# Placing the side matmuls of the full-attention layers by an estimate of two engines' clocks

## The chip, the core and the metric

The kernel runs on one NeuronCore of a Trainium2 chip. The metric is the device time of one execution in microseconds (us); lower is better. Five engines run their own instruction queues in order: TensorE (PE in the profile, its weight loads PEld), VectorE (DVE), ScalarE (ACT), GpSimd (POOL) and SyncE (SP, which here only issues transfers). An engine waits for another through semaphores, and whatever stands behind a waiting instruction in its queue waits too.

## The reference

Four pre-norm attention layers follow each other on a sequence of 2048 rows of 512 features, with 32 heads of 16 features. Layers 0 and 2 attend within a window of 256 keys, layers 1 and 3 to all keys. There is no MLP.

```python
def _B_ref(x, wqkv, wo):
    qkv = (x @ wqkv).reshape(B, S, 3, H, Dh).transpose(2, 0, 3, 1, 4)
    q, k, v = qkv[0], qkv[1], qkv[2]
    scores = jnp.einsum("bhqd,bhkd->bhqk", q, k) * Dh ** -0.5
    p = _softmax(scores, axis=-1)
    o = jnp.einsum("bhqk,bhkd->bhqd", p, v)
    return o.transpose(0, 2, 1, 3).reshape(B, S, D) @ wo
# _A_ref is the same with scores outside 0 <= query - key < 256 masked out
x = x + _A_ref(_layernorm(x), A_wqkv, A_wo)     # layer 0
x = x + _B_ref(_layernorm(x), B_wqkv, B_wo)     # layer 1
x = x + _A_ref(_layernorm(x), A_wqkv, A_wo)     # layer 2
x = x + _B_ref(_layernorm(x), B_wqkv, B_wo)     # layer 3
```

## The kernel before

**A full layer.** Layers 1 and 3 work through 32 *quads* each: four heads (`qd`) by 512 queries (`c`). A quad takes 16 steps `j` of 128 keys. In each step TensorE computes two groups of scores (eight matmuls each, L771, tile `s`, two buffers), ScalarE turns each group into exponentials with one activation of 128x1024 (L779, tile `e`, five buffers), and TensorE later multiplies the exponentials of the step with the values (16 matmuls, L896, into the two banks `acc`; below "the value product"). Within a step TensorE's order is: first group of scores, value product of two steps before, second group of scores, and then whatever side work has been placed there. The value product is held in a list `pvq` that `flush` empties.

**The thirty-second group.** In most quads one group of scores (step `DJ`, placed last in its quad) does not go to ScalarE: `unit` (L787) computes it into `b`, VectorE turns it into an integer (L793), and GpSimd evaluates the exponential with a polynomial (L810 to L817). Such a quad has 31 activations, the others 32. `units` decides when `unit` may run.

**Side work.** The projections of later blocks (keys `keys`, queries `queries`, values `values`), the output projections (`wo`, `wo_part`) and the layer norms of the layers around run beside the attention. Their matmuls (L424) write one shared pair of PSUM banks, tile `b`, with a single buffer in the full layers. A *piece* is one pair of operands in `mms`: eight matmuls of 512 columns, planned as `MM` = 0.222 us. Twelve pieces (in `wo_part`, three) fill `b`; then VectorE reads it (`join`, or L718 and L693 for `x`), and only then may the next user write `b`. Users of `b` are the pieces, `unit`, and `squares` (L579, the sums of squares that bound the scores).

**What sets the order.** The order on TensorE, VectorE and GpSimd in the full layers is written while the program is built: nothing is rescheduled later. The planner keeps an estimated time `clock[0]` (TensorE), `vt_` (VectorE), `pt_` (GpSimd), and `PH["free"]`, the time from which `b` is taken to be readable and free. A step of the attention counts as `PH["step"]`, 1.8 us (0.9 for the step with the unit). `Side.share` decides after each group of scores how many pieces follow: it hands out a `budget` that spreads the remaining cost evenly over the remaining steps, and keeps a `lag` account (+0.222 per piece, -0.48 per step) that limits a run to one or two pieces more. `Side.finish` runs what is left at the end of a block (layer 3), or of the layer (layer 1), with no attention beside it. `settle` runs `squares` when their time has come, and `project` calls it before its first piece. `epilogue` ends a quad: VectorE reads `acc` (L440, L441, tile `sa`) before the next quad's first value product may overwrite it.

## Time and profile before

| | us |
|---|---|
| median of 3 runs (2795.52 to 2798.0) | 2796.48 |
| the profiled execution's own time | 2797.65 |
| its span in the profile | 2795.9 |
| ScalarE busy over the span | 2330.1 (83%) |
| TensorE busy over the span | 2500.0 (89%) |
| VectorE, GpSimd busy | 1445.5 (52%), 1537.5 (55%) |
| layer 1, first to last activation | 499 to 1457 |
| layer 3, first to last activation | 1812 to 2777 |
| GpSimd exponentials (L793) | 58 of 64 quads |

The profile is of one execution. A row of its timeline gives the start, the length, engine, line, operation, tile written <- tiles read, shapes and count, and in brackets how long the engine was idle before it and what ended that wait. Matmuls are pipelined: their issue is closer together than their lengths tell, so distances are read from start to start.

### The profile page before, as it was taken

The numbers are of one execution on the slowest core, as the hardware profiler recorded it, in microseconds if no ns is written. First come the engines' busy times: TensorE is split into PE (matmuls) and PEld (weight loads), VectorE is DVE, ScalarE is ACT, GpSimd is POOL, SyncE is SP. The second block draws the span as 40 slices with busy tenths as digits, with TensorE's granted clock in tenths as the row PEclk, the third lists the DMA queues.
The fourth block names the chain that finished last, engine by engine and source line by source line (L and its number), as shares of the span: only waits on it lengthen the run. The fifth ranks groups of instructions, "written<-read, shape, count | busy, mean of one in ns | idle before, by whom it ended". The sixth has DMA issues, their size and how long they took to land.

```text
span 2795.9 us, 113153 instructions
## 1 busy us (share of the span) xinstructions
PE 2500.0 (89%) x50177; PEld 1095.1 (39%) x50177; DVE 1445.5 (52%) x2725; ACT 2330.1 (83%) x2629; POOL 1537.5 (55%) x2148
## 2 busy tenths in 40 slices
PE   7789989989998999999989888899999889988987
PEld 3233434444343444344433333534444444333332
DVE  5566554234556455563656566445544454555553
ACT  4565653899999999999985667399999999999997
POOL 1455551556657354554634677186755646656673
PEclk9999999999999999999999999999999999999999
DMA  8887866222223322322336564623333333333341
GB/s 284 224 244 239 246 176 182 85 81 78 78 98 106 94 82 93 115 95 75 105 104 192 146 187 140 179 63 99 100 95 107 96 92 116 115 107 123 118 132 56
DMA packets 335044, 359.72 MB, mean 129 GB/s; under 512 B 113616, under 2 KB 250320, under 8 KB 328144
## 3 DMA queue, kind: packets, MB, share of 16 engines
q1 hardware_dynamic: 334544, 352.40, 41.8%
q8 instruction: 394, 6.46, 1.0%
q14 instruction: 106, 0.87, 0.1%
HBM read 239.60 MB, written 96.99 MB: 120 GB/s over the span
## 4 chain that ended last, share of the span: by engine, by line
ACT 50%; PE 26%; issue 11%; DVE 7%; DMA 4%; POOL 1%; SPq 1%; ACTq 0%; DVEq 0%; POOLq 0%
ACT e L779 49%; PE b L427 10%; PE acc L896 5%; PE acc L929 3%; PE s L771 2%; PE b L424 2%; PE bs L427 2%; PE s L775 2%; POOL e L919 1%; POOL e L922 1%; DMA kt<-kw 1%; DMA wo<-wd 1%; DMA x<-in_A_x_dram 0%; DVE xh L481 0%; DVE ot L737 0%
## 5 line engine op out<-in xcount | busy, mean ns | idle before, releaser
L779 ACT ACTIVATE e<-s 128x1024 f32<-128x1024 f32 (+2 forms) x2374 | 2204.9, 1044 | 184.4 <-PE s L775 112.8
L896 PE MATMUL acc<-e,vt 64*17 64x512 f32 x15920 | 1080.7, 589 | 1.9 <-DVE sa L440 1.8
L771 PE MATMUL s<-qt,kt 64*32 64x512 f16 x15920 | 835.4, 380 | 157.5 <-ACT e L779 131.9
L771 PEld LDWEIGHTS <-kt 64*32 64x32 f16 x15920 | 385.8, 89 | 911.6 <-issue 830.3
L812 POOL TENSOR_SCALAR scr<-scr 128x512 f32<-128x512 f32 x116 | 92.4, 797 | 790.5 <-DVE scr L801 785.9
L922 POOL TENSOR_SCALAR_AFFINE_SELECT e<-e 128x256 f32<-128x256 f32 x512 | 227.4, 451 | 209.7 <-ACT e L779 208.8
L815 POOL TENSOR_TENSOR scr<-scr,scr 128x512 f32<-128x512 f32 x248 | 315.9, 1295 | 9.9
L896 PEld LDWEIGHTS acc<-e,vt 64*17 64x17 f32 x15920 | 282.5, 92 | 96.6 <-issue 32.6
L810 POOL TENSOR_SCALAR scr<-scr 128x512 f32<-128x512 f32 x464 | 298.7, 644 | 37.9
L815 POOL TENSOR_TENSOR scr<-scr 128x512 f32<-128x512 f32 x216 | 279.6, 1315 | 8.7
L919 POOL TENSOR_SCALAR_AFFINE_SELECT e<-e 128x256 f32<-128x256 f32 x448 | 200.1, 453 | 110.4 <-ACT e L779 109.0
L929 PE MATMUL acc<-e,vt 128*17 128x384 f32 (+2 forms) x2816 | 202.0, 392 | 1.8 <-DVE ot L737 0.8
L427 PE MATMUL b<-xc,w 128*128 128x512 f16 x708 | 170.1, 392 | 11.8 <-DMA w<-wd 6.3
L775 PE MATMUL s<-qt,kt 64*128 64x384 f16 (+2 forms) x1408 | 127.4, 278 | 54.1 <-ACT e L779 33.6
L440 DVE TENSOR_SCALAR sa<-acc 128x512 f32<-128x512 f32 x64 | 44.1, 689 | 219.6 <-PE acc L896 214.2
L817 POOL TENSOR_TENSOR d<-scr,d 128x512 f32<-128x512 f32 x116 | 147.7, 1294 | 4.6
L440 DVE TENSOR_SCALAR j_h<-b 128x512 f32<-128x512 f32 x27 | 18.7, 691 | 211.8 <-PE b L424 211.8
L427 PEld LDWEIGHTS <-w 128*128 128x128 f16 x816 | 77.5, 100 | 128.9 <-issue 43.2
L541 ACT ACTIVATE sp<-b 128x512 f16<-128x512 f32 x59 | 35.3, 598 | 109.9 <-PE b L427 99.8
L718 DVE SCALAR_TENSOR_TENSOR x<-b,x 128x512 f32<-128x512 f32 x122 | 83.8, 687 | 78.3 <-PE b L424 74.8
L793 DVE TENSOR_SCALAR d<-b 128x1024 int32<-128x1024 f32 x58 | 71.0, 1224 | 102.4 <-PE b L787 102.4
L775 PEld LDWEIGHTS <-kt 64*128 64x128 f16 x1408 | 53.9, 94 | 155.6 <-issue 128.0
(149 smaller groups left out, 2583.5 us busy)
## 6 DMA issues: line engine op xcount, KB each, us to landing
kt<-kf SPq DMA_DIRECT2D x128, 512.0 KB
qt<-qs SPq DMA_DIRECT2D x128, 256.0 KB
xd<-x SPq DMA_DIRECT2D x96, 256.0 KB
x<-xd SPq DMA_DIRECT2D x96, 256.0 KB
w<-wd SPq DMA_DIRECT2D x22, 1024.0 KB
kt<-kw SPq DMA_DIRECT2D x64, 256.0 KB
qs<-sp SPq DMA_DIRECT2D x48, 256.0 KB
wo<-wd SPq DMA_DIRECT2D x12, 1024.0 KB
```

Source lines behind the costliest of these rows:

```text
L427: nc.tensor.matmul(ps, a, b, start=(i == 0), stop=(i == len(pairs) - 1))
L771: nc.tensor.matmul(ps[g:g + 32, h], kt[R * h:R * h + R, pr, kc + g:kc + g + 32], qt[R * h:R * h + R, pr], start=True, stop=True, skip_grou ...
L775: nc.tensor.matmul(ps[:, h, s0:s0 + wd_], kt[R * h:R * h + R, pr, kc:kc + P], qt[R * h:R * h + R, pr, qc:qc + wd_], start=True, stop=True)
L779: nc.scalar.activation(e[:, :, w0:w1], ps[:, :, w0:w1], AF.Exp, scale=SCALE)
L810: nc.gpsimd.tensor_scalar(a[h], a[h], 1.0, POLY[4 - k], op0=ALU.mult, op1=ALU.add)
L812: nc.gpsimd.tensor_scalar(a[h], f[h], POLY[5], POLY[4], op0=ALU.mult, op1=ALU.add)
L815: nc.gpsimd.tensor_tensor(a[h], a[h], f[h], ALU.mult)
L817: nc.gpsimd.tensor_tensor(x[:, h], a[h], x[:, h], ALU.mult)
L896: nc.tensor.matmul(acc[r][32 * h:32 * h + DH + 1, :], V[l, qd // 4, j // 8][k, j % 8, 4 * (qd % 4) + h, :], es_[h // 2][k, h % 2, :], star ...
L919: nc.gpsimd.affine_select(v, v, pattern=[[0, 2], [-1, P]], compare_op=ALU.is_gt, fill=0.0, base=0, channel_multiplier=1)
L922: nc.gpsimd.affine_select(v, v, pattern=[[0, 2], [1, P]], compare_op=ALU.is_ge, fill=0.0, base=0, channel_multiplier=-1)
L929: nc.tensor.matmul(a[32 * h:32 * h + DH + 1, q * P:(q + nb) * P], V[l, (4 * c + j) // 4][:, j % 4, 4 * qd + h, :], es_[h // 2][:, h % 2, s ...
```

## The change

The planner gets a second estimated clock, `AT`, a list of the times at which ScalarE will be done with each group of scores. A group of scores is planned to start no earlier than 0.05 us after the activation two before it is done (its buffer is then free), to take `SC` = 0.216 us, and its activation to take `EX` = 0.905 us from the later of ScalarE's last end and 0.2 us after the scores. `room()` is the time by which ScalarE's planned end is ahead of TensorE's planned time, less `ROOM` = 0.6 us. A side piece may follow while `room()` is at least 0.6 of a piece (0.133 us), at most three in a row; `unit` and `squares` ask for 0.1 us. The even spread (`budget`), the `lag` account and the fixed step of 1.8 us go away, so side work is placed wherever the estimate says it fits, as early as its inputs allow. The value product counts 0.87 us in place of 1.0. `join` now also moves `PH["free"]` to 0.3 us after VectorE's planned end. `PH["end"]`, which `units` compares with, follows `AT`.

```diff
+SC, EX, ROOM = 0.216, 0.905, 0.6
...
+    AT = [0.0, 0.0]
+    def room():
+        return AT[-1] - ROOM - clock[0]
...
     def join(dst, ps, scale=1 / WS):
         vec(1.4)
+        PH["free"] = max(PH["free"], vt_[0] + 0.3)
...
-        spent(0.27)
+        if PH["full"]:
+            clock[0] = max(clock[0], AT[-2] + 0.05)
+            spent(SC)
+            AT.append(max(AT[-1], clock[0] + 0.2) + EX)
+        else:
+            spent(0.27)
...
-            if not PH["busy"] and clock[0] >= PH["free"]:
+            if not PH["busy"] and clock[0] >= PH["free"] and room() >= 0.1:
                 unit(u)
...
-            spent(1.0)
+            spent(0.87 if PH["full"] else 1.0)
...
-            PH["step"] = 1.8 - 0.9 * len(es_)
...
-            self.budget = min(self.budget + max((self.cost - self.spent) / max(self.steps - 3 - self.k, 1), self.least), 0.75)
-            self.lag = max(self.lag - 0.48, -0.4)
-            if pend and not PH["busy"] and not VQ[0] and clock[0] >= max(PH["free"], pend[0][0], PH["sq"]):
+            if pend and not PH["busy"] and not VQ[0] and clock[0] >= max(PH["free"], pend[0][0], PH["sq"]) and room() >= 0.1:
                 settle(False)
                 PH["free"] = clock[0] + 2.0
-                self.lag += 0.1
             s0 = self.spent
-            while (self.q and clock[0] >= PH["free"] and self.budget >= MM / 2 and (self.lag < 0.25 or self.budget > 0.45)
-                   and self.spent - s0 < (1.5 if self.lag > 0.1 else 2.5) * MM):
+            while (self.q and clock[0] >= PH["free"] and room() >= 0.6 * MM
+                   and self.spent - s0 < 2.5 * MM):
                 c = self.one()
                 if c is None:
                     break
-                self.budget -= abs(c)
-                self.lag += abs(c)
...
-                PH["side"], PH["quad"], PH["end"] = sd, (l, c, qd), clock[0] + 1.8 * NT
+                PH["side"], PH["quad"], PH["end"] = sd, (l, c, qd), AT[-1] + 31 * EX
...
-                    clock[0] = max(clock[0], began + (2.4 if win else PH["step"]))
+                    if win:
+                        clock[0] = max(clock[0], began + 2.4)
```

The number of side matmuls is the same in both kernels, and the orders of the windowed layers 0 and 2 are the same on TensorE but for names. What moves is seen in TensorE's order in the full layers. A name reads tile, layer, block `c`, quad `qd`, step, half, and a running number; lines of the changed kernel are a few higher (L771 is L779 there, L424 is L431, L787 is L800, L896 is L908, L775 is L783).

**The end of layer 1.** Before, from the last group of scores to the first scores of layer 2; the rows left out repeat the row above them, the first gap with 263 more side matmuls of the key projection for layer 2 (`w2_1_2`):

```order
L771 MATMUL s1_3_7_7_1_28708<-qt1_3_7_27370,kt1_3_7_0_27372 32x512
...
L424 MATMUL b1_5728<-xc2_2_28070,w2_1_2_28055 32x512
...
L579 MATMUL b1_5728<-sq2_1_2_0_28650,hsum_86 32x512
...
L896 MATMUL acc0_81<-e1_3_7_14_0_28626,vt1_1_1_5656 17x512
...
L896 MATMUL acc0_81<-d1_3_7_27644,vt1_1_0_5831 17x512
...
L775 MATMUL s2_0_0_0_0_29079<-qt2_0_0_29072,kt2_0_0_29071 128x384
```

The same place with the change:

```order
L779 MATMUL s1_3_7_7_1_29099<-qt1_3_7_27801,kt1_3_7_0_27803 32x512
...
L908 MATMUL acc0_81<-e1_3_7_14_0_29048,vt1_1_1_5656 17x512
...
L908 MATMUL acc0_81<-e1_3_7_15_0_29078,vt1_1_1_5656 17x512
...
L908 MATMUL acc0_81<-d1_3_7_28410,vt1_1_0_5788 17x512
...
L783 MATMUL s2_0_0_0_0_29167<-qt2_0_0_29160,kt2_0_0_29159 128x384
```

The 264 side matmuls and eight matmuls of `squares` that stood between the layers now stand earlier, inside layer 1.

**The middle of a quad.** Layer 1, block 2, quad 2, from the second scores of step 9 to the first of step 12, before; behind the three `L424` rows shown stand 7, 23 and 15 more of the same kind:

```order
L771 MATMUL s1_2_2_9_1_19084<-qt1_2_2_17947,kt1_2_2_1_17951 32x512
...
L424 MATMUL b1_5728<-wo1_1_18355,oh1_1_7_17440 32x512
...
L771 MATMUL s1_2_2_10_1_19129<-qt1_2_2_17947,kt1_2_2_1_17951 32x512
...
L771 MATMUL s1_2_2_11_1_19163<-qt1_2_2_17947,kt1_2_2_1_17951 32x512
...
L424 MATMUL b1_5728<-wo1_1_18355,oh1_1_1_13367 32x512
...
L771 MATMUL s1_2_2_12_1_19221<-qt1_2_2_17947,kt1_2_2_1_17951 32x512
...
L424 MATMUL b1_5728<-wo1_1_18355,oh1_1_3_14683 32x512
```

With the change; at each of the two `L431` rows, a matmul and the weight load of the next such run, stand 24 side matmuls:

```order
L779 MATMUL s1_2_2_9_1_19430<-qt1_2_2_18293,kt1_2_2_1_18297 32x512
...
L800 MATMUL b1_5728<-qt1_2_3_19037,kt1_2_3_0_19039 32x512
...
L779 MATMUL s1_2_2_10_1_19470<-qt1_2_2_18293,kt1_2_2_1_18297 32x512
...
L431 MATMUL b1_5728<-xc2_0_14445,w2_0_0_16297 32x512
...
L779 MATMUL s1_2_2_11_1_19527<-qt1_2_2_18293,kt1_2_2_1_18297 32x512
...
L431 LDWEIGHTS w2_0_0_16297
```

One, none, three and two pieces in a row have become runs of three; steps without side work stand elsewhere in exchange.

**The start of a quad.** Layer 3, block 3, quad 3, from its second scores on, before (16 side matmuls stand at each of the two `L424` rows, the second of which is the weight load that opens the run):

```order
L771 MATMUL s3_3_3_0_1_44510<-qt3_3_3_43748,kt3_3_3_0_43750 32x512
...
L896 MATMUL acc0_81<-d3_3_2_43526,vt3_0_0_33000 17x512
...
L771 MATMUL s3_3_3_1_0_44538<-qt3_3_3_43748,kt3_3_3_0_43750 32x512
...
L424 MATMUL b3_33477<-xc3_0_30761,w3_0_0_h2_43811 32x512
...
L771 MATMUL s3_3_3_1_1_44565<-qt3_3_3_43748,kt3_3_3_0_43750 32x512
...
L424 LDWEIGHTS w3_0_0_h2_43811
...
L771 MATMUL s3_3_3_2_0_44592<-qt3_3_3_43748,kt3_3_3_0_43750 32x512
```

With the change:

```order
L779 MATMUL s3_3_3_0_1_44484<-qt3_3_3_43723,kt3_3_3_0_43725 32x512
...
L908 MATMUL acc0_81<-d3_3_2_43471,vt3_0_0_33088 17x512
...
L779 MATMUL s3_3_3_1_0_44508<-qt3_3_3_43723,kt3_3_3_0_43725 32x512
...
L779 MATMUL s3_3_3_1_1_44519<-qt3_3_3_43723,kt3_3_3_0_43725 32x512
...
L779 MATMUL s3_3_3_2_0_44530<-qt3_3_3_43723,kt3_3_3_0_43725 32x512
```

The pieces beside the quad's first steps, where VectorE reads `acc` for the quad before, are gone from there.

More of the change, by code (lines that the diff above doesn't have):

```diff
@@ L788, in unit @@
                                  u["qt"][R * h:R * h + R, 0], start=True, stop=True, skip_group_check=True)
-        spent(0.27)
+        spent(SC)
         vec(1.4)
@@ L1006, in __init__ @@
             self.q, self.steps, self.cost, self.spent, self.k = [], steps, 0.0, 0.0, 0
-            self.budget = self.lag = 0.0
             for w in sorted(carried + list(works), key=lambda w: PH.get("full") and w.name is None):
```

## The prediction

> **What bounds the kernel now.** I read the page's engine shares first, then the chain of waits, and then cut the span at the first and last activation of the two full layers.
>
> ```profile
> PE 2500.0 (89%) x50177; PEld 1095.1 (39%) x50177; DVE 1445.5 (52%) x2725; ACT 2330.1 (83%) x2629; POOL 1537.5 (55%) x2148
> ACT 50%; PE 26%; issue 11%; DVE 7%; DMA 4%; POOL 1%; SPq 1%; ACTq 0%; DVEq 0%; POOLq 0%
> 499.30:1457.00 957.70, 873.41 (x21928) 388.90 (x21927) 482.49 (x862) 927.93 (x998) 532.07 (x545) 1.00 0.29 90
> 1457.00:1472.80 15.80, 10.07 (x280) 4.84 (x262) 10.35 (x18) 0.03 (x1) 0.33 (x1) 1.00 0.55 183
> 1811.80:2777.20 965.40, 868.61 (x21598) 384.06 (x21601) 478.63 (x747) 925.14 (x993) 604.01 (x621) 1.00 0.33 103
> ```
>
> The windows give time, busy PE, PEld, DVE, ACT and POOL, the granted clock, DMA share and GB/s. In both full layers ScalarE is busy 927.93 of 957.70 and 925.14 of 965.40 us at a TensorE clock of 1.00: ScalarE's activations bound them, and the change, which leaves their kind alone, can win only what ScalarE idles there, about 30 and 40 us, and the 15.8 us behind layer 1 in which ScalarE does nothing. The groups by line say what the idle time is:
>
> ```profile
> L779 ACT ACTIVATE e<-s 128x1024 f32<-128x1024 f32 x997 | 927.9, 1060 | 29.8 <-PE acc L896 13.3 <-PE s L771 11.1 <-ACT e L779 1.1
> L779 ACT ACTIVATE e<-s 128x1024 f32<-128x1024 f32 x993 | 925.1, 1056 | 40.3 <-PE acc L896 20.9 <-PE s L771 13.3 <-ACT e L779 1.2
> ```
>
> (Layer 1, then layer 3.) Waits for the scores (`PE s`) are what better placing can cure. Waits for the value product (`PE acc`) are mostly something else, as ScalarE's timeline shows:
>
> ```profile
> 530.83 26.87 ACT L779 ACTIVATE e<-s 128x1024 f32<-128x1024 f32 x29 [0.27 <-PE s L771]
> 588.35 58.69 ACT L779 ACTIVATE e<-s 128x1024 f32<-128x1024 f32 x63 [0.51 <-PE acc L896]
> 647.55 28.99 ACT L779 ACTIVATE e<-s 128x1024 f32<-128x1024 f32 x31 [0.51 <-PE acc L896]
> ...
> 828.14 28.85 ACT L779 ACTIVATE e<-s 128x1024 f32<-128x1024 f32 x31 [0.51 <-PE acc L896]
> 857.51 29.06 ACT L779 ACTIVATE e<-s 128x1024 f32<-128x1024 f32 x31 [0.51 <-PE acc L896]
> 887.08 28.89 ACT L779 ACTIVATE e<-s 128x1024 f32<-128x1024 f32 x31 [0.51 <-PE acc L896]
> ```
>
> After each quad of 31 activations the next waits 0.51 us until a value product frees a buffer of `e`; behind a quad of 32 (the first row of 63 runs through) it does not. That wait comes from the odd count and stays. 26 such waits make layer 1's 13.3; 30 make 15.3 of layer 3's 20.9, which leaves 5.6. What placing can cure is thus 11.1 + 13.3 + 5.6 = 30.0 us.
>
> **Part 1, the end of layer 1.** Before, 264 side matmuls and `squares` are left over when the scores end:
>
> ```profile
> 1447.68 9.30 ACT L779 ACTIVATE e<-s 128x1024 f32<-128x1024 f32 x10
> ...
> 1453.37 0.41 PE L771 MATMUL s<-qt,kt 64*32 64x512 f16 x8 [0.35 <-ACT e L779]
> ...
> 1453.58 1.05 PE L896 MATMUL acc<-e,vt 64*17 64x512 f32 x16
> ...
> 1454.44 0.41 PE L771 MATMUL s<-qt,kt 64*32 64x512 f16 x8
> 1454.66 0.84 PE L424 MATMUL b<-xc,w 64*32 64x512 f16 x24
> ...
> 1455.30 0.41 PE L771 MATMUL s<-qt,kt 64*32 64x512 f16 x8
> 1455.52 2.14 PE L424 MATMUL b<-xc,w 64*32 64x512 f16 x72
> ...
> 1459.19 2.79 PE L424 MATMUL b<-xc,w 64*32 64x512 f16 x96 [1.53 <-DVE j L441]
> ...
> 1469.37 2.10 PE L896 MATMUL acc<-e,vt 64*17 64x512 f32 x32
> ...
> 1472.77 1.51 ACT L779 ACTIVATE e<-s 128x768 f32<-128x768 f32 x2 [15.79 <-PE s L775]
> ```
>
> From 1455.52 to 1469.37 TensorE does nothing else, and the last value products and layer 2's scores stand behind it. In the changed order nothing stands there: -13.9 us. What could be late next are layer 2's loads, whose place in SyncE's queue the change also moves:
>
> ```profile
> 1426.21 0.37 SPq L869 DMA_DIRECT2D qt<-qs  x1
> 1426.64 0.46 SPq L870 DMA_DIRECT2D kt<-kw  x1
> ```
>
> They are issued 29 us before the scores end, so they cover even an end 14 us earlier. Bounds: -13.9, and -11 if something holds layer 2 for 3 us.
>
> **Part 2, runs of three.** The moved work has to fit beside the activations. From the rows above: scores to scores with a value product between is 1454.44 - 1453.37 = 1.07 us; with a run of three, 1455.30 - 1454.44 = 0.86. A step with three pieces takes TensorE 1.93 us. ScalarE's two activations take 2 x (9.30 - 1.06) / 9 = 1.83. So a run of three makes ScalarE wait 0.10 us, each time: a step with two pieces (one piece is 0.64 / 3 = 0.21 us) takes 1.72 and costs nothing, but the lead it gains is used up by the next value product, because the scores have only two buffers. Counted over the whole of TensorE's order (both layers, without runs glued to `squares`), runs of three pieces go from 119 to 239, often in neighbouring steps, and runs of one from 159 to 16. The planner lets them through since it starts an activation 0.416 us after its scores start (0.216 + 0.2) and counts 0.905 per activation. Cost: 120 x 0.10 = +12 us. Bounds: 0 if the planned lead is there after all, +24 if a late value product doubles it.
>
> Here the Trainium skill would give another price. In "ScalarE: Activation LUTs", section "What ACT_TABLE_LOAD costs", an activation with immediate scale and bias takes 186 ns plus 0.833 ns per element, and neighbours overlap by about 93 ns: by that page, an estimate of 0.95 us for 1024 elements, 1.89 us for two, and a run of three would cost 0.04 us, +5 in all. The ten activations measured above came every 0.92 us, so the trace doesn't agree, and the sum goes by the trace.
>
> **Part 3, waits for `b` and for `acc`.** These make the 30.0 us of curable idle:
>
> ```profile
> 2264.11 0.84 PE L424 MATMUL b<-xc,w_h 64*32 64x512 f16 x24 [1.97 <-DVE km L598]
> ...
> 2266.14 1.02 ACT L779 ACTIVATE e<-s 128x1024 f32<-128x1024 f32 x1 [2.83 <-PE acc L896]
> ```
> ```profile
> 2548.81 1.40 DVE L718 SCALAR_TENSOR_TENSOR x<-b,x 128x512 f32<-128x512 f32 x2
> 2550.27 0.84 PE L424 MATMUL b<-xc,w_h 64*32 64x512 f16 x24 [2.33 <-DVE x L718]
> 2551.45 1.02 ACT L779 ACTIVATE e<-s 128x1024 f32<-128x1024 f32 x1 [2.27 <-PE s L771]
> ```
> ```profile
> 1369.99 1.44 PE L896 MATMUL acc<-e,vt 64*17 64x512 f32 x9 [0.97 <-DVE sa L440]
> ```
>
> Three kinds. In the first, a projection's first piece stands directly behind `squares` and waits for VectorE to read `b` (1.97), or `squares` stand directly behind the last piece. `project` forces this, and the order still has it: three and three before, three and two with the change, and one new place where two jobs of `wo_part` follow without a gap. Six places at about 1.6 us of ScalarE's time make 9.6. In the second, VectorE was late with `b`. `join` now pushes `PH["free"]` behind VectorE's planned end, and in the order short gaps near a quad's start are gone; but `wo_part` (L718) does not call `join`, so I leave 4 us. In the third, the next quad's value product waits because VectorE reads `acc` late; fewer pieces stand there now, but VectorE's order decides it: 5 us stay. The 0.27 us behind a unit in step 1 (530.83) goes, since units now stand in steps 4 and later. 18.6 of 30.0 stay: -11.4 us. Bounds: 0 and -30.
>
> **Part 4, units and the last quad.** Four more quads have a unit (58 to 62). Each removes an activation but adds the odd-count wait: 62 activations took 887.08 - 828.14 = 58.94 us, 63 took 647.55 - 588.35 = 59.20. A unit is worth 0.26 us, four make -1.0, not the 3.7 of four activations. GpSimd's extra work lies beside (604 of 965 us busy). In layer 3 the changed order has two jobs of `wo_part`, 48 matmuls, between the last scores and the last value products, where nothing stood:
>
> ```profile
> 2775.39 0.41 PE L771 MATMUL s<-qt,kt 64*32 64x512 f16 x8 [0.35 <-ACT e L779]
> 2775.61 1.91 PE L896 MATMUL acc<-e,vt 64*17 64x512 f32 x32
> ...
> 2778.48 0.69 DVE L440 TENSOR_SCALAR sa<-acc 128x512 f32<-128x512 f32 x1 [9.07 <-PE acc L896]
> ```
>
> Two runs at 0.64, and between them VectorE's two reads (1.40, above) with some 0.3 to start: +3.0 us. Bounds +1.3 and +4.
>
> **The sum** against the profiled execution's own 2797.65 us: -13.9 + 12 - 11.4 - 1.0 + 3.0 = -11.3, or 2786.3. The median shown is 1.2 us lower, which would make 2785.2; I say **2786**. Steps without pieces and steps with one swap places at much the same cost, and I count them at nothing.
>
> **Rivals.**
> *TensorE is the bound in bursts and waits inside them.* Side jobs now follow each other as soon as the estimate allows, and each change of user of `b` (253 in the new order) could wait for VectorE at the head of TensorE's queue, with scores and value products behind it. At 0.1 us each that is +25 on the sum: 2811, slower. It decides from (11.3 + 5.6) / 253 = 0.07 us on. For it: the waits of 2 us above. Against it: most changes still have two steps between them, 3.7 us, against VectorE's 1.4.
> *Nothing comes out of it.* Runs of three cost double (0.20, by delaying the value product that frees `e`), and the end of layer 1 gains 11: -11 + 24 - 11.4 - 1 + 3 = +3.6, 2801, no change. For it: neighbouring runs of three, which the trace of before hardly has. Against it: the arithmetic of a step doesn't depend on the step before.
> *All curable waits go and the runs fit.* -13.9 + 0 - 26 - 1 + 3 = -38, 2760. For it: the planner now counts both engines. Against it: six forced places remain in the order.
>
> The page of the Trainium skill named above, "ScalarE: Activation LUTs", would put the sum between the forecast and this rival: +5 for the runs in place of +12, 2779; the trace's spacing of 0.92 us speaks against it.
>
> *The change doesn't do what it says*, because its clock isn't ScalarE's: it plans 31 x 0.905 = 28.1 us per quad, the trace has 29.4 (828.14 to 857.51). Then side work is only done earlier, waits stay: -13.9 + 12 - 1 + 3 = 0, 2797.
>
> **Chances.** Forecast 0.62 (its own range 2779 to 2793); no gain, by either of the two rivals at 2797 and 2801, 0.20; slower 0.10; much faster 0.08. Two executions of this kernel are told apart from about 0.2% on, 5.6 us. Some 0.06 of the forecast's own range lies within that bound: faster 0.64, same 0.25, slower 0.11. The range from the bounds of the parts: 2774 to 2799.
>
> **What would show it.** Right: ScalarE's idle time behind layer 1 falls from 15.79 to about 2 us; `PE s` waits before activations fall from 24.4 to some 12 to 15 us in both layers while activations' own spacing grows, 31 of them taking 29.2 rather than 28.9 us where runs of three stand; 0.51 us waits at 60 quad starts; the last value products begin about 3 us later behind layer 3's last scores. Wrong: layer 2's first scores waiting for `kt` or `qt`; rows of `b` (L431) that wait for VectorE more often than before; layer 1 longer than 957.7 us by more than 15.

## The result and the profile after

The changed kernel takes 2790.19 us (median of 20 runs, 2785.18 to 2797.48) where the kernel before takes 2798.92 (20 runs, 2793.93 to 2804.88): ratio 0.9971, 95% interval 0.9963 to 0.9979, so 0.29% faster, 8.7 us. The profiled execution was the slowest of its 20 (2797.48), so a second profile of the same kernel, from an execution of 2786.55 us, stands beside it below.

The page's engine shares and chain of the changed kernel, and the windows from the first to the last activation of layer 1, the gap behind it, and layer 3 (time, then busy PE, PEld, DVE, ACT and POOL, granted clock, DMA share, GB/s):

```profile
PE 2486.5 (89%) x50177; PEld 1112.7 (40%) x50177; DVE 1466.0 (52%) x2741; ACT 2334.7 (84%) x2625; POOL 1612.0 (58%) x2228
ACT 49%; PE 26%; issue 10%; DVE 8%; DMA 4%; POOL 1%; SPq 0%; ACTq 0%; DVEq 0%
```
```profile
499.70:1464.00 964.30, 874.97 (x22176) 402.50 (x22171) 517.85 (x895) 929.07 (x993) 609.74 (x625) 0.99 0.30 92
1464.00:1465.70 1.70, 1.70 (x29) 0.45 (x18) 0.36 (x1) 0.05 (x2) 0.33 (x1) 1.00 1.00 308
1806.00:2773.90 967.90, 860.66 (x21542) 391.35 (x21534) 472.40 (x744) 928.35 (x993) 602.93 (x621) 1.00 0.33 101
```

The gap behind layer 1 has shrunk from 15.8 to 1.7 us; the two layers have not become shorter (957.7 and 965.4 before), although layer 1 has four activations fewer. The groups of activations by line (busy, mean ns of one, then ScalarE's idle time before them and what ended it), layer 1 and layer 3 of the first profile:

```profile
L792 ACT ACTIVATE e<-s 128x1024 f32<-128x1024 f32 x993 | 929.1, 1051 | 35.6 <-PE acc L908 16.0 <-PE s L779 14.1 <-ACT e L792 0.9
L792 ACT ACTIVATE e<-s 128x1024 f32<-128x1024 f32 x993 | 928.3, 1050 | 40.3 <-PE acc L908 21.5 <-PE s L779 14.8
```

and of the second:

```profile
L792 ACT ACTIVATE e<-s 128x1024 f32<-128x1024 f32 x993 | 929.0, 1050 | 33.3 <-PE acc L908 16.0 <-PE s L779 11.9 <-ACT e L792 0.9
L792 ACT ACTIVATE e<-s 128x1024 f32<-128x1024 f32 x993 | 928.4, 1049 | 37.5 <-PE acc L908 19.9 <-PE s L779 13.7
```

The waits for scores (`PE s`), 24.4 us before, are 28.9 and 25.6: they have not gone. What the end of layer 1 gave was partly given back inside the layers.

**A finer count.** Idle time alone is not enough here. An activation lasts 1.05 us and the next starts about 0.91 us behind it, so a delay of up to 0.14 us shows in no idle column. I therefore took from the trace the starts of all activations of the two layers, subtracted 0.909 us for each (an estimate of the distance without a delay: in every profile the distances cluster near 0.904 and 0.92 us), and put the excess of each step, counted from the last activation of the step before, down to what TensorE's order has there. In the first step of a quad all of it counts as "quad start"; in the second and third, where it is over 0.45 us, as "early stall"; of the rest, steps with a spacing over 1.3 us, with `squares` or with the unit's matmuls make "other stalls". Sums over layers 1 and 3, us, one profile each:

| | before | changed, 1st profile | changed, 2nd profile |
|---|---|---|---|
| steps with three pieces | 9.9 | 22.9 | 23.5 |
| steps with fewer | 17.1 | 13.2 | 13.5 |
| quad starts | 54.1 | 58.0 | 56.2 |
| early stalls | 10.5 | 14.7 | 13.8 |
| other stalls | 22.0 | 17.6 | 14.9 |
| sum | 113.6 | 126.4 | 121.9 |

With four activations fewer (-3.6), the gap behind layer 1 (-14.1) and the end of layer 3 (+3.1) this gives -1.8 and -6.3 us for the two profiles. The two executions themselves took 0.2 and 11.1 us less than the profiled one of before, and the medians differ by 8.7. Of what the second profile leaves, 5.0 us lie ahead of layer 1, where nothing was changed: its first activation starts at 499.36 before, at 499.71 and 494.35 in the two profiles of the one changed kernel, and between 493.9 and 501.9 in all the profiles used here. One profile is thus good for some 5 us, so differences below that are taken from the timed rounds.

### The profile page after: what moved, and what is told of

The parts are those of the page before. It is cut to its first block, busy times and chain, and to the rows that moved or that the text cites. A ratio compares the mean times of both kernels' runs of the same rounds, so it can differ in the third digit from the quotient of the medians.

```text
span 2795.7 us, 113278 instructions
## 1 busy us (share of the span) xinstructions
PE 2486.5 (89%) x50177; PEld 1112.7 (40%) x50177; DVE 1466.0 (52%) x2741; ACT 2334.7 (84%) x2625; POOL 1612.0 (58%) x2228
## 4 chain that ended last, share of the span: by engine, by line
ACT 49%; PE 26%; issue 10%; DVE 8%; DMA 4%; POOL 1%; SPq 0%; ACTq 0%; DVEq 0%
ACT e L792 49%; PE b L434 10%; PE acc L908 5%; PE acc L941 3%; PE s L779 3%; PE b L431 2%; PE s L783 2%; PE bs L434 1%; POOL e L934 1%; POOL e L931 1%; DMA kt<-kw 1%; DVE x L726 1%; DVE xh L489 1%; DVE xn L479 0%; DMA x<-in_A_x_dram 0%
## 5 line engine op out<-in xcount | busy, mean ns | idle before, releaser
L908 PE MATMUL acc<-e,vt 64*17 64x512 f32 x15888 | 1085.7, 591 | 5.7 <-DVE sa L448 5.3
L779 PE MATMUL s<-qt,kt 64*32 64x512 f16 x15888 | 838.3, 380 | 177.3 <-ACT e L792 155.7
L779 PEld LDWEIGHTS <-kt 64*32 64x32 f16 x15888 | 375.7, 90 | 894.1 <-issue 814.1
L825 POOL TENSOR_SCALAR scr<-scr 128x512 f32<-128x512 f32 x124 | 98.7, 796 | 734.2 <-DVE scr L814 729.2
L823 POOL TENSOR_SCALAR scr<-scr 128x512 f32<-128x512 f32 x496 | 320.6, 646 | 40.6
L908 PEld LDWEIGHTS acc<-e,vt 64*17 64x17 f32 x15888 | 287.1, 93 | 113.3 <-issue 39.0
L828 POOL TENSOR_TENSOR scr<-scr 128x512 f32<-128x512 f32 x248 | 317.7, 1302 | 10.0
L783 PE MATMUL s<-qt,kt 64*128 64x384 f16 (+2 forms) x1408 | 127.6, 279 | 54.5 <-ACT e L792 32.8
L448 DVE TENSOR_SCALAR sa<-acc 128x512 f32<-128x512 f32 x64 | 44.1, 690 | 231.8 <-PE acc L908 226.4
L830 POOL TENSOR_TENSOR d<-scr,d 128x512 f32<-128x512 f32 x124 | 159.5, 1308 | 5.0
L448 DVE TENSOR_SCALAR j_h<-b 128x512 f32<-128x512 f32 x27 | 18.7, 692 | 199.1 <-PE b L431 199.1
L783 PEld LDWEIGHTS <-kt 64*128 64x128 f16 x1408 | 54.0, 95 | 156.2 <-issue 127.6
```

Of the source, the lines that this page charges most:

```text
L779: nc.tensor.matmul(ps[g:g + 32, h], kt[R * h:R * h + R, pr, kc + g:kc + g + 32], qt[R * h:R * h + R, pr], start=True, stop=True, skip_grou ...
L783: nc.tensor.matmul(ps[:, h, s0:s0 + wd_], kt[R * h:R * h + R, pr, kc:kc + P], qt[R * h:R * h + R, pr, qc:qc + wd_], start=True, stop=True)
L823: nc.gpsimd.tensor_scalar(a[h], a[h], 1.0, POLY[4 - k], op0=ALU.mult, op1=ALU.add)
L828: nc.gpsimd.tensor_tensor(a[h], a[h], f[h], ALU.mult)
L830: nc.gpsimd.tensor_tensor(x[:, h], a[h], x[:, h], ALU.mult)
L908: nc.tensor.matmul(acc[r][32 * h:32 * h + DH + 1, :], V[l, qd // 4, j // 8][k, j % 8, 4 * (qd % 4) + h, :], es_[h // 2][k, h % 2, :], star ...
```

## The experiments

All were timed in five rounds, in three sittings whose medians of the kernel before were 2800.82, 2799.18 and 2798.39 us; each ratio goes against its own sitting. Where medians of two sittings are subtracted below, the difference by the ratios can be up to 3 us another. Four expectations count the units wrong, as the numbers of activations show (2048 less those of the two layers): the kernel before has 58 and not 57, the one without the line in `join` 62 and not 60, and the last two runs have 61 and 59 and not 57.

**The changed kernel once more.**

> The changed kernel once more, for a second profile: the one at hand is of an execution of 2797.5 us, 7 us above the kernel's median. Theory A (the forecast's terms: end of layer 1 -13.9, runs of three +12, end of layer 3 +3, fewer waits, units nothing): 2786 to 2792 us, ScalarE's gap behind layer 1 again 1.7 us, runs of three again about 0.10 us each, and the 5.5 us wait for the value product in one quad start gone or much smaller. Theory B (the waits on VectorE are worse with the change, and that execution shows it): those waits at quad starts come again at the same quads and of the same size, 13 us in layer 1.

2791.31 us (11 runs), ratio 0.9964 (0.9952 to 0.9976). It gave the second profile above. Each theory held in part. The time, the gap behind layer 1 (1.65 us of wait) and the cost of a run of three are as in A. But the waits at quad starts came again at the same quads, as in B: the longest, 5.54 us in the first profile, is 5.57 us in the second, and the early stalls of layer 1 sum to 13.5 and 12.6 us. They belong to the kernel and not to one slow execution.

**The end of layer 1 put back.** In `Side.share`:

```diff
             s0 = self.spent
+            if self.steps > 300 and self.cost - self.spent < 9.4:
+                return
```

> The changed kernel with its last 30 pieces and the squares of layer 1 held back until the scores of the layer are done, as before the change. Theory A: the end of layer 1 was the one large gain, so this costs 12.5 to 14 us and the time is 2802 to 2805, slower than before the change by about 4. Rival (what follows layer 1 is held by something else, loads or VectorE, and the gain came from elsewhere): under 5 us more than the changed kernel.

2808.68 us, ratio 1.0027 (1.0018 to 1.0037): 17.4 more than the changed kernel in the same sitting, above the 12.5 to 14 that were expected. ScalarE's timeline (start, length, and in brackets the wait):

```profile
1457.13 7.50 ACT L792 ACTIVATE e<-s 128x1024 f32<-128x1024 f32 x8
1480.55 1.51 ACT L792 ACTIVATE e<-s 128x768 f32<-128x768 f32 x2 [15.92 <-PE s L783]
```

against, in the second profile of the changed kernel:

```profile
1439.07 17.55 ACT L792 ACTIVATE e<-s 128x1024 f32<-128x1024 f32 x19
1458.28 1.51 ACT L792 ACTIVATE e<-s 128x768 f32<-128x768 f32 x2 [1.65 <-PE s L783]
```

The wait differs by 14.3 us. In this profile another 2.8 us lie behind layer 3's last activation (25.7 us from its start to the end of the span, against 22.9), although the order there is the same; whether other executions of this run have them is not shown. Without this piece the change is a loss.

**Without the line in `join`.**

```diff
     def join(dst, ps, scale=1 / WS):
         vec(1.4)
-        PH["free"] = max(PH["free"], vt_[0] + 0.3)
```

> The changed kernel without the line in join that moves the time from which b is taken to be free behind VectorE's planned end. Theory A: waits for b come back near quad starts, +4 to +7 us, less 3 us since in this order no side work is left behind layer 3's last scores and less 3 to 5 us since two squares and one wo_part job are no longer glued to the job ahead: about -2 to +2. Theory B (the line is what keeps TensorE from waiting): +8 us or more.

2799.80 us, ratio 0.9997 (0.9985 to 1.0009): 8.5 us lost, as theory B has it. Layer 1, layer 3, from the slowest of its 12 executions:

```profile
L791 ACT ACTIVATE e<-s 128x1024 f32<-128x1024 f32 x993 | 930.0, 1053 | 42.1 <-PE s L778 19.4 <-PE acc L907 16.4 <-PE b L431 0.7
L791 ACT ACTIVATE e<-s 128x1024 f32<-128x1024 f32 x993 | 927.8, 1053 | 45.3 <-PE s L778 23.1 <-PE acc L907 17.9
```

Waits for scores are 42.5 us in place of 25.6. The line is what keeps pieces from waiting for VectorE's read of `b` at the head of TensorE's queue (18.7 us of such waits without it, 9.0 and 10.4 with it, by the count at the end of the next section). It costs the two jobs of `wo_part` at the end of layer 3 (this kernel has none there and gains 3 us), and pays for them.

**Without units.** `units` returns before it places one, so all 1024 groups of a layer go to ScalarE:

```diff
             if u["e"] or clock[0] < u["ready"]:
                 continue
+            return False
```

> The changed kernel without any score group on GpSimd: all 1024 groups of each full layer go to ScalarE, and GpSimd has no work in the full layers. Theory A as forecast (a unit is worth 0.26 us, since it brings the odd-count wait with it): 62 x 0.26 = +16 us. Theory C (GpSimd's work lengthens VectorE's instructions, and these delay the value product at quad starts): the 0.51 us waits go, the early waits of a quad go too, VectorE's sums and differences in SBUF take their short time everywhere, and the time is +3 us or less, or faster.

2767.70 us, ratio 0.9885 (0.9865 to 0.9905): 62 activations more, and 23.6 us less, where theory A had 16 more. ScalarE's timeline of layer 1, whole, and both layers' groups:

```profile
494.06 4.79 ACT L792 ACTIVATE e<-s 128x1024 f32<-128x1024 f32 x5
500.02 237.23 ACT L792 ACTIVATE e<-s 128x1024 f32<-128x1024 f32 x256 [1.17 <-PE s L779]
737.65 212.87 ACT L792 ACTIVATE e<-s 128x1024 f32<-128x1024 f32 x229 [0.40 <-PE s L779]
950.69 495.88 ACT L792 ACTIVATE e<-s 128x1024 f32<-128x1024 f32 x534 [0.17 <-PE s L779]
```
```profile
L792 ACT ACTIVATE e<-s 128x1024 f32<-128x1024 f32 x1024 | 950.2, 1054 | 2.3 <-PE s L779 1.7
L792 ACT ACTIVATE e<-s 128x1024 f32<-128x1024 f32 x1024 | 949.0, 1052 | 7.3 <-PE s L779 6.4
```

Four rows hold all 1024 activations. Waits for `acc` are gone, and nearly all waits for scores as well. In the finer count, quad starts fall from 56.2 to 1.6 us (54.6, or 0.88 for each of 62 units), the two kinds of stalls from 28.7 to 9.5. Against these 73.8 us stand 62 x 0.909 = 56.4 of activations. The end of layer 3 gives another 3.5, since no job of `wo_part` is left there.

**The kernel before without units.** The same line in the kernel before.

> This is the kernel before with all 1024 groups of a full layer left to ScalarE: GpSimd and VectorE take none of the exponentials, nothing is left out of the result. Theory (the price of a unit is the same in both kernels): a unit takes one activation away (0.905 us), and leaves an odd number of single scores, so that the next quad's first activation waits, and it keeps GpSimd busy beside VectorE. In the kernel before the 57 units save 57 x 0.905 = 51.6 us of activations, and cost 52.5 us at the starts of quads (54.1 us of excess spacing less the 1.6 us that the run without units kept), 8.5 us of stalls in the next two steps and 4.5 us at the units themselves: 13.9 us net. Also no side work is left behind layer 1's last scores in its order, which takes the 15.79 us of idle ScalarE to some 1.7: 14.1 us. 2798.9 - 13.9 - 14.1 gives about 2771, 3 us above the 2767.7 of the changed kernel without units. Rival (the clocks in the place of the lag account are worth 8.7 us whatever else runs): 2767.7 + 8.7, about 2776. Second rival (runs of three pieces, 110 here where the changed kernel without units has 237, decide once the units are gone): 2767.7 - 12.7, about 2755.

2775.34 us, ratio 0.9917 (0.9903 to 0.9930), at the rival's 2776. Layer 1, layer 3:

```profile
L779 ACT ACTIVATE e<-s 128x1024 f32<-128x1024 f32 x1024 | 946.5, 1061 | 12.2 <-PE s L771 11.2
L779 ACT ACTIVATE e<-s 128x1024 f32<-128x1024 f32 x1024 | 945.8, 1062 | 13.3 <-PE s L771 12.3
```

Neither of these two kernels has side work behind layer 1's last scores. Between them lies what the new placing does by itself: waits for scores from 23.5 to 8.1 us, stalls in the early and other steps from 28.9 to 9.5; steps with three pieces up by 14.8 (8.6 to 23.4). The medians differ by 7.6 us (9 by the ratios). That this is near the 8.7 of the kernels with units is chance: 14 us of those came from the end of layer 1, where nothing is to be won here. Without units the waits do go.

**Two pieces at most, in layer 1, without units.**

```diff
-                   and self.spent - s0 < 2.5 * MM):
+                   and self.spent - s0 < (1.5 if PH["quad"][0] == 1 else 2.5) * MM):
```

> The changed kernel without units, and in layer 1 a step takes at most two side pieces in place of three (300 steps of two, none of three, where there were 124 and 111); layer 3 as it was. Nothing is left out. Theory (a step with three pieces costs ScalarE 0.10 us, a step with two nothing): 111 x 0.10 = 11 us come off layer 1, 951.4 us from its first to its last activation become about 940, the time 2767.7 becomes about 2757; layer 3 stays at 955. Rival (TensorE is simply full where pieces are dense, and what a run of three costs a run of two costs in another place): layer 1 stays within 3 us of 951, the time within 3 us of 2768.

2764.99 us, ratio 0.9879 (0.9863 to 0.9895); the interval of the changed kernel without units, 0.9865 to 0.9905, overlaps this one, so the time alone doesn't tell. The layer does. The windows of layers 1 with three pieces, from the kernel without units, and with two:

```profile
494.00:1446.60 952.60, 865.07 (x22184) 406.15 (x22175) 345.65 (x771) 950.28 (x1025) 0.84 (x3) 1.00 0.31 93
```
```profile
499.10:1442.80 943.70, 877.96 (x22184) 395.74 (x22175) 345.87 (x771) 942.84 (x1024) 0.78 (x3) 1.00 0.31 94
```

The same 22184 matmuls and 1024 activations take 8.9 us less when no step has three pieces. There were 111 such steps: 0.08 us each, net of what steps with two now cost. Layer 3, which was left alone, took 3.6 us more than in the other profile. So the layer bears the theory out, at 8.9 of the forecast 11 beside 3.6 of difference in a layer that is the same in both, and the time of the whole kernel neither confirms nor refutes it.

**A value product after the single score.** A step whose other group went to the unit has one score pair, and handed out no value product. On the kernel without the line in `join`:

```diff
-                if pr == 0:
+                if pr == 0 or j == DJ and len(es_) == 2 and u["e"]:
                     yield None
```

> As the changed kernel without its line in join (2799.8 us, 60 units), but the step after a unit, which has one score pair in place of two, hands out its value product by itself too, so that the next quad does not start one short; 61 units; nothing is left out. Theory (the waits at quad starts come from the odd number of scores): of the 54 us of excess spacing at quad starts most goes, since the run without units has 1.6 there: if two thirds go, 36 us, and the time is about 2764. Rival (the wait at a quad's start is the lateness of VectorE with what the first value product needs, which GpSimd's chain brings about): 2795 to 2803. In between, each has its part.

2762.50 us, ratio 0.9874 (0.9858 to 0.9890): 37.3 less than 2799.80 (34 by the ratios), with 36 forecast. Layer 1, layer 3, here from the fastest of its four executions:

```profile
L791 ACT ACTIVATE e<-s 128x1024 f32<-128x1024 f32 x993 | 926.4, 1054 | 19.8 <-PE s L778 15.4 <-ACT e L791 0.6
L791 ACT ACTIVATE e<-s 128x1024 f32<-128x1024 f32 x994 | 926.1, 1052 | 27.3 <-PE s L778 22.2 <-ACT e L791 1.7
```

The waits for `acc`, 16.4 and 17.9 us without this line, are no longer among the causes listed. Quad starts in the finer count fall from 54.2 to 16.6; in the other profiles with 58 to 62 units and without this line they lie between 54 and 58. Two thirds of the wait at a quad's start come from an odd number of scores with one value product too few behind them.

**Units in their own quad alone.**

```diff
-            if u["e"] or clock[0] < u["ready"]:
+            if u["e"] or clock[0] < u["ready"] or u["quad"] != PH["quad"]:
```

> The changed kernel, but a unit may only be given out while its own quad runs: 22 units in the two layers in place of 62, each of them early enough that GpSimd has ended before the quad does. Nothing is left out. Theory (what a unit costs is the odd number of scores, some 0.87 us at the next quad's start, and beside this VectorE's work at the boundary that GpSimd makes longer; the second part is not there now): 22 x (0.87 - 0.905) on the 2767.7 us of the kernel without units, about 2767. Rival (a unit costs its net 23.6 / 62 = 0.38 us wherever it stands): 2767.7 + 22 x 0.38, about 2776.

2787.67 us, ratio 0.9965 (0.9952 to 0.9978): both theories fall, since each of the 22 units costs 0.9 us net (1.0 by the ratios). Layer 1, layer 3:

```profile
L792 ACT ACTIVATE e<-s 128x1024 f32<-128x1024 f32 x1014 | 944.4, 1050 | 11.0 <-PE acc L908 5.4 <-PE s L779 2.1 <-ACT e L792 0.3
L792 ACT ACTIVATE e<-s 128x1024 f32<-128x1024 f32 x1012 | 942.6, 1049 | 29.3 <-PE s L779 18.0 <-PE acc L908 6.4 <-ACT e L792 0.7
```

Quad starts were forecast right (20.0 us, 0.91 per unit), but the units' own steps cost 8.5 us here (1.3 for all 62 in the changed kernel), and the early and other stalls beside them 16.7 (9.5 without units). The trace shows what the 8.5 are: all 22 units stand in the first step of their quad, where a value product follows the second scores, and with the unit between them TensorE needs 1.29 us from scores to scores (585.33 to 586.62 in one such step), more than the 0.91 between two activations. Each costs 0.3 to 0.39 us. In the changed kernel units stand in later steps, where the next scores follow directly, and most cost 0.02. So the price of a unit depends on its place, and the first step of its quad is a worse one. What the other stalls come from was not followed further.

**GpSimd's work made narrow.** Each of the polynomial's instructions on the first 32 of 512 columns, in an order that is otherwise the changed kernel's:

```diff
-                    nc.gpsimd.tensor_tensor(a[h], a[h], f[h], ALU.mult)
+                    nc.gpsimd.tensor_tensor(a[h][:, :32], a[h][:, :32], f[h][:, :32], ALU.mult)
```

> The changed kernel in its own order, but GpSimd's polynomial of a unit runs over the first 32 columns of each half alone, in place of 512: the other columns of the unit's exponentials keep only their power of two, so the output is not the reference's there. Nothing else is moved. Theory (GpSimd's instructions make VectorE's longer, VectorE is late with what the quad's first value products need, and this gives the stalls in the second and third step of a quad): these 13.8 us of excess spacing go, with about half of the 7.2 us of other stalls, and the waits at quad starts, which come from the odd number of scores, stay at some 54; the time is 2791 - 16, about 2775. Rival (VectorE is late by its own queue, and GpSimd only runs at the same time): within 3 us of 2791. Second rival (the waits at quad starts come from GpSimd too): they fall by more than half, 2791 - 16 - 30, about 2745.

2768.68 us, ratio 0.9891 (0.9876 to 0.9906): 22.6 us less than the changed kernel's 2791.31 (20 by the ratios), more than the 16 forecast. Layer 1, layer 3:

```profile
L792 ACT ACTIVATE e<-s 128x1024 f32<-128x1024 f32 x993 | 928.4, 1051 | 22.8 <-PE acc L908 16.0 <-PE s L779 1.3 <-ACT e L792 0.9
L792 ACT ACTIVATE e<-s 128x1024 f32<-128x1024 f32 x993 | 926.4, 1050 | 30.4 <-PE acc L908 20.2 <-PE s L779 6.8
```

Waits for `acc` at the starts stay, 36.2 us; waits for scores fall from 25.6 to 8.1. In the finer count quad starts stay at 56.4, early stalls go from 13.8 to 0.5, other stalls from 14.9 to 10.3. The two costs of a unit are thus separate: the narrow GpSimd takes away the stalls, the hand-out after the single score the waits at the starts.

How the stalls come about is seen at one quad's start of the changed kernel, first profile:

```profile
1069.45 5.02 ACT L792 ACTIVATE e<-s 128x1024 f32<-128x1024 f32 x5 [0.51 <-PE acc L908]
...
1071.56 0.97 DVE L559 TENSOR_TENSOR sp<-j,sp 128x512 f16<-128x512 f32 x1
1072.08 2.99 POOL L828 TENSOR_TENSOR scr<-scr 128x512 f32<-128x512 f32 x2
1072.46 1.49 DVE L564 TENSOR_TENSOR sq<-sp 128x512 bf16<-128x512 f16 x1
...
1073.87 1.48 DVE L479 TENSOR_SCALAR xn<-x,mv,y 128x512 f32<-128x512 f32 x1
...
1076.03 0.67 DVE L448 TENSOR_SCALAR sa<-acc 128x512 f32<-128x512 f32 x1
...
1076.76 2.72 PE L908 MATMUL acc<-e,vt 64*17 64x512 f32 x16 [3.65 <-DVE sa L448]
...
1080.01 1.02 ACT L792 ACTIVATE e<-s 128x1024 f32<-128x1024 f32 x1 [5.54 <-PE s L779]
```

VectorE reads `acc` (L448) 6.6 us after the quad's first activation, behind instructions that took longer than they need: L564 1.49 us and L479 1.48, with GpSimd narrow at most 0.42 and 0.57, and L559 0.97 in place of 0.69. TensorE's first value product of the quad waits for that at the head of its queue, the next scores stand behind it, and ScalarE idles 5.54 us. VectorE's rows by line in layer 1 (minimum, median, maximum ns; first and last start; shapes), changed kernel, second profile:

```profile
L559 DVE TENSOR_TENSOR sp<-j,sp x28: 691/834/1662, 634.6 to 1438.8; 128x512 f16<-128x512 f32 x28
L564 DVE TENSOR_TENSOR sq<-sp x28: 412/420/1486, 636.2 to 1440.4; 128x512 bf16<-128x512 f16 x28
L763 DVE CAST oh<-o x15: 426/1346/1473, 559.3 to 1404.4; 128x512 f16<-128x512 f32 x15
L448 DVE TENSOR_SCALAR sa<-acc x31: 671/691/693, 525.7 to 1429.4; 128x512 f32<-128x512 f32 x31
```

and with GpSimd narrow:

```profile
L559 DVE TENSOR_TENSOR sp<-j,sp x28: 691/692/693, 635.9 to 1427.0; 128x512 f16<-128x512 f32 x28
L564 DVE TENSOR_TENSOR sq<-sp x28: 417/419/421, 636.5 to 1427.6; 128x512 bf16<-128x512 f16 x28
L763 DVE CAST oh<-o x16: 426/427/522, 560.4 to 1452.3; 128x512 f16<-128x512 f32 x16
```

Instructions that work from SBUF alone have a tail of up to 1.66 us that goes with GpSimd's load; L448, which reads PSUM, has none. In neither profile does VectorE wait for an instruction of GpSimd, so what makes it late are its own longer instructions.

**The hand-out after a single score, in the kernel before.** The same line as above.

> The kernel before, its even spread and its lag account, with the one line that lets the step after a unit hand out its value product by itself. 57 units as before; 200 passes and eight of the squares stay behind layer 1's last scores (264 before). Nothing is left out. Theory (the odd number of scores costs the same in both kernels): 36 us come off, as they did from the changed kernel without its line in join (2799.8 to 2762.5), and the tail is some 3 us shorter: 2799 - 39, about 2760, so that this line alone is worth more than the whole change. Rival (the old account places side work into the steps that this line changes, and the waits only turn up elsewhere): 2780 or more.

2787.47 us, ratio 0.9953 (0.9939 to 0.9967): 11 us (13 by the ratio) in place of 39, with three units more than the kernel before. Layer 1, layer 3:

```profile
L779 ACT ACTIVATE e<-s 128x1024 f32<-128x1024 f32 x994 | 923.7, 1060 | 31.0 <-PE s L771 27.3 <-ACT e L779 0.5
L779 ACT ACTIVATE e<-s 128x1024 f32<-128x1024 f32 x993 | 924.4, 1058 | 37.4 <-PE s L771 33.4
```

The waits for `acc` have gone here too, but waits for scores rose from 24.4 to 60.7 us. In the finer count quad starts fall by 20 us, to 33.7, and the early and other stalls rise by 19. The rival holds: with the old account the waits turn up elsewhere. Which rule of it does that stays open.

**The three together.** The changed kernel with the hand-out, and

```diff
-SC, EX, ROOM = 0.216, 0.905, 0.6
+SC, EX, ROOM = 0.216, 0.905, 0.75
...
-        PH["free"] = max(PH["free"], vt_[0] + 0.3)
+        PH["free"] = max(PH["free"], vt_[0] - 1)
```

> The changed kernel with three numbers and lines moved: the step after a unit hands out its value product by itself; the line in join claims 1.0 us before VectorE's estimated end in place of 0.3 us behind it, so that nothing is left behind the layers' last scores; and the margin ROOM is 0.75 in place of 0.6, which leaves 219 steps with three pieces (239 in the changed kernel). 57 units, nothing is left out. Theory (the prices add up): from the 2762.5 of the run with this hand-out and no line in join, 2 us come off for the runs of three and some 5 of the 31.7 us of stalls in the early and other steps, since the line in join took 17 us off them in the changed kernel: 2755 to 2760. Rival (the smaller claim of the line in join does nothing for the waits): 2762 or a little more.

2759.98 us, ratio 0.9854 (0.9839 to 0.9869): 38.4 us below the kernel before and the lowest median of all that were run, at the upper end of the 2755 to 2760 forecast. Layer 1, layer 3:

```profile
L792 ACT ACTIVATE e<-s 128x1024 f32<-128x1024 f32 x994 | 923.8, 1050 | 20.5 <-PE s L779 17.0 <-ACT e L792 0.4
L792 ACT ACTIVATE e<-s 128x1024 f32<-128x1024 f32 x995 | 925.3, 1050 | 30.2 <-PE s L779 26.0 <-ACT e L792 0.3
```

Its interval overlaps that of the kernel with the hand-out and no line in `join` (0.9858 to 0.9890), and the waits for scores are 43.0 us here against 37.6 there, in one profile each. So it is not shown that the weaker claim helps, nor that the prices add up as the theory has it.

## Why the prediction was right in sign and where it failed

The forecast was 2786 and faster; measured were 2790.19 and faster. By steps, with the two profiles of the changed kernel:

| step | predicted | measured |
|---|---|---|
| Part 1, end of layer 1 | -13.9 | -14.1, -14.1 |
| Part 2, runs of three | +12 | +13.0, +13.6 |
| steps with fewer pieces | 0 | -3.9, -3.6 |
| Part 3, waits (early and other stalls) | -11.4 | -0.2, -3.8 |
| Part 4, four more units | -1.0 | +0.3, -1.5 |
| Part 4, end of layer 3 | +3.0 | +3.1, +3.1 |

**Part 1** was right in mechanism and size, and putting the work back confirms it. Layer 2's scores waited 1.65 us and not for their loads.

**Part 2** was right: a step with three pieces costs 0.1 us. The row of 31 activations that was to grow from 28.9 to 29.2 us did (second profile):

```profile
764.16 29.14 ACT L792 ACTIVATE e<-s 128x1024 f32<-128x1024 f32 x31 [0.51 <-PE acc L908]
793.81 29.24 ACT L792 ACTIVATE e<-s 128x1024 f32<-128x1024 f32 x31 [0.51 <-PE acc L908]
823.57 5.02 ACT L792 ACTIVATE e<-s 128x1024 f32<-128x1024 f32 x5 [0.51 <-PE acc L908]
829.36 23.94 ACT L792 ACTIVATE e<-s 128x1024 f32<-128x1024 f32 x26 [0.77 <-PE s L779]
```

Such a row alone is weak evidence: the first of these has four steps with three pieces, the second has two and is longer. The count over all steps carries the reading. Taking the steps with three pieces out of layer 1 gave 0.08 each. That neighbouring runs would cost double (the rival at 2801) is not so: 88 of them, right behind another, cost 0.107 each.

**Part 3** failed, at the sentence on the third kind: "fewer pieces stand there now, but VectorE's order decides it: 5 us stay". The last two rows above are such a start: five activations, then a wait. VectorE's order alone was not what decided: in the same order, with GpSimd's instructions narrow, the early stalls are 0.5 us in place of 13.8. I counted "GpSimd's extra work lies beside" and did not ask what it does to VectorE. VectorE's scaling of `op`, which follows its reading of `acc`, overlaps an instruction of GpSimd in 52 of 62 quads now, in 33 of 62 before: with the units in their new places GpSimd's chain runs across the quad's boundary more often. The early stalls rose by 3 to 4 us where they were to fall. That the overlaps are the reason fits the narrow run; no run moves the units' places alone. The second kind did fall, as far as `join` reaches: without its line the waits for scores are 17 us longer in the profiles, and the kernel 8.5 us. Without units the step is right as put: stalls go from 28.9 to 9.5 us. What was wrong was to take those waits as a matter between TensorE and VectorE alone.

**Part 4.** That the 0.51 us wait "comes from the odd count and stays" was right, and a one-line test of its cause took it away. The price of a unit was wrong: 0.26 us gained was read from quads that had only this wait. Over all 62 a unit loses some 0.28 us in the layers: quad starts cost 0.88 on average and the stalls 0.31 (19.2 / 62), against the 0.91 that it saves; with the end of layer 3 the 23.6 us make 0.38. For four more units that made little; it hid that the units, which I took as given, were the largest cost beside the change. The end of layer 3, second profile:

```profile
2761.08 0.41 PE L779 MATMUL s<-qt,kt 64*32 64x512 f16 x8 [0.28 <-ACT e L792]
...
2761.30 0.84 PE L431 MATMUL b<-wo,oh 64*32 64x512 f16 x24
...
2763.68 0.84 PE L431 MATMUL b<-wo,oh 64*32 64x512 f16 x24 [1.54 <-DVE x L726]
...
2764.32 1.91 PE L908 MATMUL acc<-e,vt 64*17 64x512 f32 x32
...
2767.20 0.69 DVE L448 TENSOR_SCALAR sa<-acc 128x512 f32<-128x512 f32 x1 [1.19 <-PE acc L908]
```

From the last scores to the last value products are 3.24 us (0.22 before), as put.

**The sum** forecast -11.3 us, and the medians differ by 8.7. Of the 4 us between 2786 and 2790, 1.3 to 2.4 are that the kernel before has a median of 2798.92 over 20 runs, and not the 2796.48 to 2797.65 that the forecast started from. By the steps of the table the two profiles give -1.8 and -6.3: an error of 8 to 11 us in Part 3 was partly met by the 4 us of the steps with fewer pieces, which I had counted at nothing, and what is left lies outside the steps counted. So the total came closer than its parts, and that was in part luck. The rival of bursts (2811) fell: the time for which side pieces stand at the head of TensorE's queue for VectorE, summed over the two layers by the view of one line's waits, is 14.3 us before, 9.0 and 10.4 in the two profiles of the changed kernel, and 18.7 without the line in `join`.

## What to carry to other kernels

Before placing work better, ask what the waits consist of: here the whole change of placing was worth 8 to 9 us, and one value product handed out a step earlier 34 to 37 on the changed kernel without its line in `join`, but only 11 to 13 on the kernel before. An engine that takes work off the bottleneck is priced by everything it disturbs: the odd count that it leaves behind, and the engine whose instructions it lengthens, not by its own idle time. And where neighbours overlap, read distances from start to start, since delays shorter than the overlap stand in no idle column.

## What the hardware showed that was not expected

Instructions of VectorE that work from SBUF alone grew by up to 1.1 us while GpSimd ran 128x512 instructions, and the reading of `acc` from PSUM didn't: a difference of two tiles took 691 ns at its shortest and 1662 at its longest (L559), a cast 426 to 1473 (L763), against 671 to 693 for the reading of `acc` (L448); with GpSimd narrow the first took 691 to 693. The Trainium skill, "SBUF — State Buffer", section "SBUF: two separate sides", says that VectorE and GpSimd share one pair of ports as an exclusive lock that is held for a whole instruction, when VectorE's has two inputs in SBUF or runs in a mode that uses two ports. By that rule the rows agree for L559 and L564; L763, with one input, grew as well, and no run here shows in which mode it ran.
